# Attention with softmax sums by DMA: K and Q copies one every two tiles, other tiles added by DMA, late raw weights two heads later

## The chip, the cores and the metric

The kernel runs on one core of one Trainium2 chip. The metric is the device time of one execution in microseconds. An engine is named as in the profile: PE is TensorE, DVE VectorE, ACT ScalarE, POOL GpSimd, SP SyncE, which here only issues DMAs.

## The reference

The output mixes two branches on the same input x (2048 tokens, 1024 features) by a gate per token. Branch A is attention with 32 heads of 32 features; branch B picks one expert of 64 for each of 32 router heads. All inputs are float32.

```python
x = A_x
g = _sigmoid((x * gate_w).sum(-1, keepdims=True))
a = _A_ref(x, A_wqkv, A_wo)
b = _B_ref(x, B_w_q, B_k1, B_k2, B_u, B_v)
return g * a + (1 - g) * b

def _A_ref(x, wqkv, wo):
    qkv = (lambda x, *d: x.transpose(*d))((x @ wqkv).reshape(B, S, 3, H, Dh), 2, 0, 3, 1, 4)
    q, k, v = qkv[0], qkv[1], qkv[2]
    scores = jnp.einsum("bhqd,bhkd->bhqk", q, k) * (Dh ** -0.5)
    p = _softmax(scores, axis=-1)
    o = jnp.einsum("bhqk,bhkd->bhqd", p, v)
    return (lambda x, *d: x.transpose(*d))(o, 0, 2, 1, 3).reshape(B, S, D) @ wo
```

## The kernel before

The program has three stages. Up to about 630 us it computes Q and K (stored to DRAM as a high and a low part), the router, the branch of the experts and the values. From there to about 1630 us it runs attention, head by head. The last 180 us multiply the heads' results by wo, with the gate, and store the output. The change touches attention only.

**One head.** A head h has 16 key tiles (kt 0 to 15) of 128 keys; a tile P[h, kt] holds exp of the scores of these keys against all 2048 queries, 128 x 2048 float32, 1 MB. Scores are matmuls of K and Q tiles of 98 rows (three parts of 32 rows and a shift of 2 rows), 512 queries each, into a ring of seven PSUM banks (line 1284). ScalarE takes exp from the ring into P (line 1296). Then `pv` multiplies P by the values into O[h] (line 1308). These run in batches: 9 or 10 score matmuls, then four or five half tiles of products, seven pairs of them in a head. The third batch of a head is the only one of ten.

**The sums of a softmax row** need all 16 tiles added up and then summed over the partitions. `presum(h, kt)` adds one tile: VectorE adds most of them into ACC[h] (line 1342, two halves of 1024 columns each), and the tiles named in `SUMS` go into ACCD[h] instead, the first of them by being written there (ACCD[h] is that P tile itself), the others by an accumulating DMA that GpSimd issues (line 1330). Such a DMA waits for the tile, for the one before it into the same ACCD, and the first of a head also until the products have read the tile that ACCD is. `merge4` adds ACC and ACCD on VectorE. For the first 24 heads (`FOURS` = 6 groups of four), `fold4` and `fold4_end` then add quarters of 32 partitions onto each other by GpSimd's DMAs, so that T (the tile rb) holds four heads in its four quarters, and `head_sums` sums a whole group over the partitions with one set of matmuls into the ring (line 1321). From head 24 on pairs are folded instead of fours, by one DMA for each head.

**Buffers.** ACC and ACCD have two buffers each. P tiles have 11 places at first; from a given call of `p_tile` on 9, then 8, since the last three places are tiles (wo_raw3, wo_raw2, vhl) that later hold weights for the last stage. `PLACES` names the calls, `LATE` the heads at which those weights are loaded, `until` is a guess of when a place comes free, by which the next place is chosen.

**The order of the work.** Instructions are written out by hand for each engine; an engine takes its own in order, and starts one when what it depends on is done. `at(step, f)` puts a call into the list `todo` of a step; step h * 16 + kt is reached in the program after the batch in which the scores of that tile are complete, and the step's list comes ahead of that tile's `presum`. SP issues nearly all plain DMAs in program order, each on one of eight semaphores in turn, so it also waits until the DMA eight before has landed. In a head it issues the six copies of 32 rows of K and Q and the shift for the next head (`load_head`, 256 KB a copy, from DRAM into the buffer that the head before used), the store of O (`finish`, od<-osb), a part of the values (`load_v`), and in some heads a raw weight of wo (`load_wo`, 256 KB). After a group of four it also stores the sums (smd<-ssb, four DMAs), loads them again (`load_r`, rr<-smd) and stores their reciprocals (`norm_r`, rd<-rr).

The steps around the change, counted from a head's step 0: K and Q of the next head at -1; store of the head before at 0; merge of the head before at 3, its first folds at 5, its last at 10, and the rowsum of the group that ended two heads before at 2. Adds by DMA at 3, 8 and 12.

Of the kernel before, what the change touches and what calls it, by code (L numbers as in the profile page):

```python
# [19 lines left out]
H = 32  # L20
KC = D // 128
HC = KC // 2
NT = S // 128
# [9 lines left out]
def gated_mha_peer_kernel(ctx, tc, xT, wqkv, wv, wo, wq, k12, ug, v, out):  # L33
# [48 lines left out]
    def dma(dst, src, queue=nc.sync):  # L82
        a, b = (ap.bitcast(F32) if ap.dtype == F32R else ap for ap in (dst, src))
        return queue.dma_start(a, b)
# [179 lines left out]
        evac_hi(*args)  # L264
        evac_lo()

    def load_kq(h, tiles):
        K, Q = tiles
        rows = slice(32 * h, 32 * h + 32)
        (qh, ql), (kh, kl) = (tuple(t[rows, :] for t in parts) for parts in QKD)  # L270
        for tile_, srcs in ((K, (kh, kh, kl)), (Q, (qh, ql, qh))):
            for i, src in enumerate(srcs):
                dma(tile_[32 * i:32 * i + 32, :], src)

    def load_shift(h, tiles):
        dma(tiles[1][96:98, :], SHD[h])
# [429 lines left out]
    for blk, (k, n) in enumerate(order):  # L706
        w, c = chunks[k]
        t = pairs[k % 2]
# [441 lines left out]
    P, pools, keep = {}, {}, None  # L1150


    SUMS = (1, 3, 8, 12), (2, 4, 6)
    PLACES = (11, 0), (9, 28 * 11), (8, 28 * 11 + 12 * 9)
    LATE = 21, 28
    until = [0] * PLACES[0][0]

    def p_tile(h, kt):


        n = [places for places, k in PLACES if pools["next"] >= k][-1]
        pools["next"] += 1
        i = min(range(n), key=lambda i: until[i])
        until[i] = h * NT + kt + (14 if kt in SUMS[h == H - 1] else 4)
        pool, name = ((pools["right"], f"P{i}") if i < 4 else (pools["left"], f"P{i}") if i < 8 else
                      (keep, ("vhl", "wo_raw2", "wo_raw3")[i - 8]))
        P[h, kt] = pool.tile([128, S], F32, name=name)
        return P[h, kt]
# [102 lines left out]
    def scores(s0, s1):  # L1271


        n = s1 - s0
        banks = ring_banks(n)
        cuts = {c for c in range(1, n + 1) if c == n or (s0 + c) % NQ == 0 or banks[c] == 0}
        cuts |= set(range(1, max(1, n - NB) + 1))
        if n <= 2 * NQ:
            cuts |= {c + 2 for c in range(NQ, n, NQ) if not cuts & {c + 1, c + 3}}
        c0 = 0  # L1280
        for c, i in enumerate(banks):
            (h, kt), qc = divmod((s0 + c) // NQ, NT), (s0 + c) % NQ
            K, Q = KQ[h % 2]
            on_ring(nc.tensor.matmul(ring[:, i, :], K[:98, kt * 128:(kt + 1) * 128],  # L1284
                                     Q[:98, qc * 512:(qc + 1) * 512], start=True, stop=True), i)
            if c + 1 not in cuts:
                continue
            m = c + 1 - c0
            q0 = qc + 1 - m
            if q0 == 0:  # L1290
                if kt == SUMS[h == H - 1][0]:
                    P[h, kt] = ACCD[h] = wk.tile([128, S], F32, name="accd")
                else:
                    p_tile(h, kt)
            i -= m - 1
            on_ring(nc.scalar.activation(  # L1296
                P[h, kt][:, q0 * 512:(q0 + m) * 512].rearrange("p (a m) -> p a m", a=m),
                ring[:, i:i + m, :], AF.Exp, scale=SCALE), *range(i, i + m))
            c0 = c + 1
# [23 lines left out]
                                       start=(src is srcs[0]), stop=(src is srcs[-1]))  # L1323

    def presum(h, kt):
        sums = SUMS[h == H - 1]
        if kt == 0 or kt == sums[0] or (h == H - 1 and kt >= NT - 2):
            return
        if kt in sums:
            nc.gpsimd.dma_start(ACCD[h], P[h, kt], accum_op=OP.add)  # L1330
            return
        if kt == 1 + (sums[0] == 1):
            if h > 0:
                ACC[h] = wk.tile([128, S], F32, name="acc")
            add(ACC[h], P[h, 0], P[h, kt])
        else:
            add(ACC[h], ACC[h], P[h, kt])

# [131 lines left out]
    def at(step, f, *a):  # L1470
        todo.setdefault(step, []).append((f, a))

    for h in range(H):
        base = h * NT
        g, j = divmod(h, 4)
        if h >= 1 and h + 1 < H:
            at(base - 1, load_head, h + 1)
        if h < H - 1:
            at(base + NT, finish, h)
            if h == H - 2:  # L1480
                at(base + NT + 5, merge, h)
                at(base + NT + 8, head_sums, h)
            elif g < FOURS:
                at(base + NT + 3, merge4, h)
                at(base + NT + 5, fold4, h)
                at(base + NT + 10, fold4_end, h)
            else:
                at(base + NT + 3, (merge_even, merge_odd)[h % 2], h)
                at(base + NT + 5, (fold_even, fold_odd)[h % 2], h)
                if h % 2:  # L1490
                    at(base + NT + 12, head_sums, h - 1, 2)
        if j == 3 and g + 1 < G:
            if g < FOURS:
# [335 lines left out]
```

## Time and profile before

| | us |
|---|---|
| three runs | 1816.46, 1820.94 (median), 1826.25 |
| the profiled execution, its own time | 1816.36 |
| its span, first to last instruction | 1814.6 |
| an ordinary head of attention | 31.0 |
| attention, 32 heads | about 1000 |
| the last stage after it | about 180 |

The profile is of one execution. Its groups are named by line, engine and out<-in with the program's names: ring<-z,z and ring<-Q,K are scores, P<-ring their exp (into the places wo_raw and vhl too), o<-P,V the products, acc<-acc,P VectorE's adds, accd<-P the adds by DMA, rb<-acc,accd and acc<-acc,accd the merge, acc<-acc, rb<-acc and rb<-rb at lines 1384 to 1393 the folds, z<-kdh and K<-kdh (and qdh, kdl, qdl) the copies of K and Q. Queue q0 carries GpSimd's DMAs, q1 those of SP. PE is busy for 99% of the span, so where time can be won or lost is seen in the few stretches in which it isn't.

### The profile page before, as it was taken

What the parts mean: (1) busy time and instruction counts of PE and PEld (TensorE: products, weight loads), DVE (VectorE), ACT (ScalarE), POOL (GpSimd) and SP (SyncE); (2) the same over time, 40 slices, a digit from 0 to 9 for tenths busy, and PEclk for the clock granted to TensorE, in tenths of its full rate; (3) what the DMA queues carried; (4) which work ended last, traced back from release to release, by engine and by line L of the source; (5) the groups of instructions that cost most, each with busy time, mean ns of one, the idle gap of its engine ahead of it and who ended that gap; (6) DMA issues with size and microseconds to landing.
All of it is one profiled execution on the core that took longest, in us unless ns stands there. A gap on an engine that the chain in (4) does not pass through costs nothing.

```text
span 1814.6 us, 28137 instructions
## 1 busy us (share of the span) xinstructions
PE 1803.1 (99%) x10631; PEld 1137.4 (63%) x10631; DVE 1499.4 (83%) x1673; ACT 1221.6 (67%) x1615; POOL 261.4 (14%) x314
## 2 busy tenths in 40 slices
PE   9999999999999999999999999999999999999999
PEld 7777777788888754455554545554454555547887
DVE  7868785368987789998999998899889999995674
ACT  4434422211243499999999999999998999993221
POOL 0222000026401211111111111111111110101000
PEclk9999999999999999999999999999999999999999
DMA  7788888723248689999999999999998998967851
GB/s 240 235 283 259 265 264 306 252 70 106 82 144 275 228 195 201 192 191 204 196 212 194 213 191 204 184 205 193 184 219 172 204 204 191 207 141 236 272 167 58
DMA packets 132226, 364.74 MB, mean 201 GB/s; under 512 B 17541, under 2 KB 57877, under 8 KB 106169
## 3 DMA queue, kind: packets, MB, share of 16 engines
q0 software_dynamic: 22064, 136.07, 37.9%
q1 hardware_dynamic: 89864, 190.94, 34.7%
q10 hardware_dynamic: 20160, 35.92, 7.0%
q8 instruction: 84, 1.38, 0.3%
q14 instruction: 54, 0.43, 0.1%
HBM read 169.14 MB, written 72.10 MB: 133 GB/s over the span
## 4 chain that ended last, share of the span: by engine, by line
PE 91%; DMA 5%; DVE 2%; issue 1%; ACT 0%; SPq 0%; POOL 0%; ACTq 0%; DVEq 0%; POOLq 0%
PE ring L1284 25%; PE o L1308 22%; PE bk L157 13%; PE bk L713 10%; PE pa L157 6%; PE bk L760 5%; PE pa L1573 2%; PE bk L928 2%; DMA accd<-P 2%; PE bk L313 2%; PE bk L493 1%; DVE acc L1342 1%; DMA rb<-acc 1%; PE pa L1580 1%; PE bk L397 1%
## 5 line engine op out<-in xcount | busy, mean ns | idle before, releaser
L1296 ACT ACTIVATE P<-ring 128x512 f32<-128x512 f32 (+3 forms) x895 | 730.8, 939 | 12.9 <-PE ring L1284 4.9
L1342 DVE TENSOR_TENSOR acc<-acc,P 128x1024 f32<-128x1024 f32 x508 | 583.6, 1217 | 4.9 <-ACT P L1296 4.7
L1308 PE MATMUL o<-P,V 128*32 128x512 f32 (+1 forms) x3624 | 378.0, 531 | 0.0
L1284 PE MATMUL ring<-Q,K 98*128 98x512 f32 x1024 | 270.6, 407 | 3.3 <-ACT P L1296 3.3
L1284 PE MATMUL ring<-z,z 98*128 98x512 f32 x1020 | 267.7, 406 | 0.1
L1284 PEld LDWEIGHTS ring<-Q,K 98*128 98x128 f32 x1024 | 182.8, 188 | 124.6 <-issue 36.6
L1284 PEld LDWEIGHTS ring<-z,z 98*128 98x128 f32 x1020 | 182.1, 188 | 116.2 <-issue 39.9
L1308 PEld LDWEIGHTS o<-P,V 128*32 128x32 f32 x3624 | 100.4, 109 | 191.2 <-issue 171.1
L1330 POOL DMA_DIRECT2D accd<-P x81 | 72.1, 891 | 505.8 <-ACT P L1296 237.4
L1296 ACT ACTIVATE wo_raw<-ring 128x512 f32<-128x512 f32 (+3 forms) x144 | 114.2, 864 | 3.0 <-PE ring L1284 1.6
L1342 DVE TENSOR_TENSOR rb<-acc,accd 32x1024 f32<-32x1024 f32 (+2 forms) x60 | 70.7, 1217 | 54.4 <-DMA accd<-P 29.5
L242 ACT ACTIVATE hi<-bk 128x512 fp32r<-128x512 f32 x40 | 23.7, 595 | 114.2 <-PE bk L713 95.2
L713 PE MATMUL bk<-xh,e 128*128 128x512 f32 x384 | 94.2, 394 | 0.0
L713 PE MATMUL bk<-xl,e 128*128 128x512 f32 x384 | 92.2, 389 | 0.0
L1296 ACT ACTIVATE vhl<-ring 128x512 f32<-128x512 f32 (+3 forms) x106 | 85.5, 872 | 2.1 <-PE ring L1284 0.7
L713 PEld LDWEIGHTS bk<-xh,e 128*128 128x128 f32 x384 | 71.0, 188 | 22.0 <-issue 3.4
L255 DVE TENSOR_TENSOR lo<-bk,hi 128x512 fp32r<-128x512 f32 x40 | 27.5, 689 | 66.8 <-ACT hi L242 61.6
L713 PEld LDWEIGHTS bk<-xl,e 128*128 128x128 f32 x384 | 72.1, 188 | 15.0
L1342 DVE TENSOR_TENSOR acc<-acc,wo_raw 128x1024 f32<-128x1024 f32 x68 | 79.8, 1218 | 0.3 <-ACT wo_raw L1296 0.3
L103 DVE TENSOR_TENSOR e<-wraw,e 128x512 fp32r<-128x512 f32 (+3 forms) x64 | 54.8, 864 | 28.3 <-ACT e L102 27.7
L1342 DVE TENSOR_TENSOR acc<-acc,vhl 128x1024 f32<-128x1024 f32 x62 | 72.9, 1217 | 0.0
L102 ACT ACTIVATE e<-wraw 128x512 fp32r<-128x512 f32 (+3 forms) x64 | 44.7, 705 | 39.1 <-DMA wraw<-in_wqkv 23.4
(305 smaller groups left out, 2550.2 us busy)
## 6 DMA issues: line engine op xcount, KB each, us to landing
accd<-P POOLq DMA_DIRECT2D x81, 1024.0 KB, 11.2
wqt<-in_wq SPq DMA_DIRECT2D x26, 1024.0 KB
wraw<-in_wqkv SPq DMA_DIRECT2D x30, 512.0 KB
rb<-acc POOLq DMA_DIRECT2D x36, 256.0 KB, 7.9
accd<-wo_raw POOLq DMA_DIRECT2D x9, 1024.0 KB, 10.2
qdh<-hi ACTq DMA_DIRECT2D x32, 256.0 KB
qdl<-lo ACTq DMA_DIRECT2D x32, 256.0 KB
kdh<-hi ACTq DMA_DIRECT2D x32, 256.0 KB
```

The lines of the kernel that those rows point to most:

```text
L102: nc.scalar.activation(hi, src, AF.Copy)
L103: (on or nc.vector).tensor_tensor(out=lo, in0=src, in1=hi.bitcast(F32), op=OP.subtract)
L157: nc.tensor.matmul(ps, self.a[a][i][:, k, :], self.b[b][j][k], start=(not first and k == 0 and i == j == 0), stop=(k == HC - 1 and i == 1))
L313: nc.tensor.matmul(ps[32 * quad:32 * quad + 32, :], kpad[:, quad % 2, i, :], t[:, quad, :], start=(i == 0), stop=(i == 3))
L713: nc.tensor.matmul(ps, t[:, kc // HC, a, kc % HC], x_at(b, n, kc), start=first, stop=last)
L760: nc.tensor.matmul(ps, x_at(a, t // 4, kc)[:, tok], b, start=first, stop=last)
L928: nc.tensor.matmul(p, x_at(a, t // 4, kc)[:, tok], b, start=first, stop=last)
L1284: on_ring(nc.tensor.matmul(ring[:, i, :], K[:98, kt * 128:(kt + 1) * 128], Q[:98, qc * 512:(qc + 1) * 512], start=True, stop=True), i)
L1296: on_ring(nc.scalar.activation(P[h, kt][:, q0 * 512:(q0 + m) * 512].rearrange("p (a m) -> p a m", a=m), ring[:, i:i + m, :], AF.Exp, scale ...
L1308: nc.tensor.matmul(O[h][32 * qc:32 * qc + 32, c0:c1], Vt[g][:, kt, 32 * j:32 * j + 32], p[:, qc * 512 + c0:qc * 512 + c1], start=(kt == 0) ...
L1330: nc.gpsimd.dma_start(ACCD[h], P[h, kt], accum_op=OP.add)
L1342: nc.vector.tensor_add(out[:, c], a[:, c], b[:, c])
```

## The change

- `load_kq` can issue single pieces. The six copies for the next head are put at steps -1, 1, 3, 5, 7 and 9 of a head and the shift at 10, in place of all seven at -1.
- For heads 1 to 30, `SUMS` is (0, 2, 6, 10): ACCD is tile 0, and tiles 2, 6 and 10 are added to it by DMA. Before it was tile 1 with 3, 8 and 12. Head 0 keeps (1, 3, 8, 12), head 31 keeps (2, 4, 6). ACC starts with the first two of the other tiles, now 1 and 3, before 0 and 2.
- Merge, first folds and last fold of a head go to steps 4, 6 and 11 of the next head, before 3, 5 and 10; the rowsum of a group of four stays. So the last fold comes after the third add of its head in GpSimd's order, where it came between the second and the third.
- The raw weights that were loaded in heads 21 to 28 are loaded in heads 23 to 30 (`LATE`), and the P tiles go from 11 places to 9 at call 338 of `p_tile` (in head 22) in place of 308 (in head 20).

```diff
-    def load_kq(h, tiles):
+    def load_kq(h, tiles, pieces=range(6)):
         K, Q = tiles
         rows = slice(32 * h, 32 * h + 32)
         (qh, ql), (kh, kl) = (tuple(t[rows, :] for t in parts) for parts in QKD)
-        for tile_, srcs in ((K, (kh, kh, kl)), (Q, (qh, ql, qh))):
-            for i, src in enumerate(srcs):
-                dma(tile_[32 * i:32 * i + 32, :], src)
+        places = [(t, i, src) for t, srcs in ((K, (kh, kh, kl)), (Q, (qh, ql, qh)))
+                  for i, src in enumerate(srcs)]
+        for n in pieces:
+            t, i, src = places[n]
+            dma(t[32 * i:32 * i + 32, :], src)
...
-    SUMS = (1, 3, 8, 12), (2, 4, 6)
-    PLACES = (11, 0), (9, 28 * 11), (8, 28 * 11 + 12 * 9)
-    LATE = 21, 28
+    SUMS = (1, 3, 8, 12), (0, 2, 6, 10), (2, 4, 6)
+    PLACES = (11, 0), (9, 338), (8, 28 * 11 + 12 * 9)
+    LATE = 23, 28
+
+    def sums_of(h):
+        return SUMS[(h > 0) + (h == H - 1)]
...
-        sums = SUMS[h == H - 1]
-        if kt == 0 or kt == sums[0] or (h == H - 1 and kt >= NT - 2):
+        sums = sums_of(h)
+        first, second = [t for t in range(NT) if t not in sums][:2]
+        if kt == first or kt == sums[0] or (h == H - 1 and kt >= NT - 2):
             return
...
-        if kt == 1 + (sums[0] == 1):
+        if kt == second:
             if h > 0:
                 ACC[h] = wk.tile([128, S], F32, name="acc")
-            add(ACC[h], P[h, 0], P[h, kt])
+            add(ACC[h], P[h, first], P[h, kt])
...
         if h >= 1 and h + 1 < H:
-            at(base - 1, load_head, h + 1)
+            for i in range(6):
+                at(base - 1 + 2 * i, load_kq, h + 1, KQ[(h + 1) % 2], [i])
+            at(base + 10, load_shift, h + 1, KQ[(h + 1) % 2])
...
             elif g < FOURS:
-                at(base + NT + 3, merge4, h)
-                at(base + NT + 5, fold4, h)
-                at(base + NT + 10, fold4_end, h)
+                at(base + NT + 4, merge4, h)
+                at(base + NT + 6, fold4, h)
+                at(base + NT + 11, fold4_end, h)
             else:
-                at(base + NT + 3, (merge_even, merge_odd)[h % 2], h)
-                at(base + NT + 5, (fold_even, fold_odd)[h % 2], h)
+                at(base + NT + 4, (merge_even, merge_odd)[h % 2], h)
+                at(base + NT + 6, (fold_even, fold_odd)[h % 2], h)
                 if h % 2:
-                    at(base + NT + 12, head_sums, h - 1, 2)
+                    at(base + NT + 13, head_sums, h - 1, 2)
```

In `p_tile` and `scores` the lookups `SUMS[h == H - 1]` become `sums_of(h)`.

More of the change, by code (lines that the diff above doesn't have):

```diff
@@ L1163, in p_tile @@
         i = min(range(n), key=lambda i: until[i])
-        until[i] = h * NT + kt + (14 if kt in SUMS[h == H - 1] else 4)
+        until[i] = h * NT + kt + (14 if kt in sums_of(h) else 4)
         pool, name = ((pools["right"], f"P{i}") if i < 4 else (pools["left"], f"P{i}") if i < 8 else
@@ L1290, in scores @@
             if q0 == 0:
-                if kt == SUMS[h == H - 1][0]:
+                if kt == sums_of(h)[0]:
                     P[h, kt] = ACCD[h] = wk.tile([128, S], F32, name="accd")
```

## The prediction

> **What bounds the kernel now.** I read the busy shares first, then the chain of work that ended last by engine, then windows of a head's length (an ordinary one and the worst), then the waits inside the worst.
>
> ```profile
> PE 1803.1 (99%) x10631; PEld 1137.4 (63%) x10631; DVE 1499.4 (83%) x1673; ACT 1221.6 (67%) x1615; POOL 261.4 (14%) x314
> PE 91%; DMA 5%; DVE 2%; issue 1%; ACT 0%; SPq 0%; POOL 0%; ACTq 0%; DVEq 0%; POOLq 0%
> 758.60:789.70 31.10, 31.10 (x223) 15.30 (x221) 28.29 (x25) 30.36 (x40) 5.15 (x7) 1.00 0.94 202
> 1350.20:1381.40 31.20, 27.91 (x184) 13.46 (x183) 25.02 (x23) 25.69 (x31) 4.90 (x6) 0.95 0.89 172
> ```
>
> TensorE is busy without a gap in an ordinary head (31.10 of 31.10 us, window row: length, PE, PEld, DVE, ACT, POOL, granted clock, DMA share). The change touches attention alone and removes no matmul, so it can only win back stalls. A usable clock for them is the third batch of scores, ten matmuls, once in every head; I call its start M. From the chain in order of time:
>
> ```profile
> 789.73 2.71 PE ring L1284 x10
> 945.74 2.59 PE ring L1284 x10
> 976.70 2.59 PE ring L1284 x10
> 1101.59 2.59 PE ring L1284 x10
> 1164.36 2.71 PE ring L1284 x10
> 1290.52 2.70 PE ring L1284 x10
> 1420.69 2.71 PE ring L1284 x10
> ```
>
> A head is 30.96 us (945.74 to 976.70). From 789.73 to 1164.36 are twelve heads, 374.63 us, 124.88 for four. The next four take 126.16 (1.28 more), the four after them 130.17 (5.29 more). So 6.57 us of stall is all there is to win in this execution. TensorE's two recorded waits, and the work before the longer:
>
> ```profile
> PE ring L1284 <- ACT P L1296: 3.3, 1, 3.3
> PE ring L1321 <- DMA rb<-acc: 0.8, 1, 0.8
> 1343.61 2.28 PE ring L1284 x9
> 1345.89 2.29 PE o L1308 x24
> 1350.06 12.19 DMA accd<-P
> 1362.35 2.36 DVE rb L1342 x2
> 1370.53 1.77 PE ring L1284 x4
> ```
>
> VectorE stood until 1362.35 at the merge of head 22, because the last accumulating DMA into accd landed late; P tiles came free late, ScalarE had no place to write, TensorE waited 3.3 us. The clock of 0.95 over that window is another 1.6 us (0.05 x 31.2). The 0.8 us is the rowsum of a group of four heads, waiting for its last fold.
>
> Why the DMA is late shows on the GpSimd queue and in the time to landing: in order the add of tile 12 of head 9; of head 10 the adds of tiles 3 and 8, the last fold of head 9's sums, and tile 12; then tile 8 of head 15.
>
> ```profile
> 934.26 0.89 POOL L1330 DMA_DIRECT2D accd<-vhl  x1 [6.50 <-ACT P L1296]
> 945.87 0.86 POOL L1330 DMA_DIRECT2D accd<-P  x1 [10.73 <-ACT P L1296]
> 957.63 0.90 POOL L1330 DMA_DIRECT2D accd<-P  x1 [6.20 <-ACT wo_raw L1296]
> 960.28 0.78 POOL L1393 DMA_DIRECT2D rb<-acc  x1 [1.76 <-DMA rb<-acc]
> 965.85 0.90 POOL L1330 DMA_DIRECT2D accd<-P  x1 [4.78 <-PE ring L1284]
> 1112.76 0.92 POOL L1330 DMA_DIRECT2D accd<-P  x1
> ```
>
> ```profile
> accd<-vhl POOLq DMA_DIRECT2D x1, 1024.0 KB, 7.2
> accd<-P POOLq DMA_DIRECT2D x1, 1024.0 KB, 11.2
> accd<-P POOLq DMA_DIRECT2D x1, 1024.0 KB, 7.7
> accd<-P POOLq DMA_DIRECT2D x1, 1024.0 KB, 10.9
> accd<-P POOLq DMA_DIRECT2D x1, 1024.0 KB, 13.9
> ```
>
> The 7.2 is of 934.26, 11.2 of 945.87, 7.7 of 957.63, 10.9 of 965.85, 13.9 of 1112.76. The three adds of a head go into one tile, so each waits for the one before: M+0.1 to M+11.3, M+11.9 to M+19.6, M+20.1 to M+31.0 in head 10, which fills the head. In head 15 the second one is behind late folds and lands at M+25.1 (1126.7). A late merge makes late folds, and these make the next merge late: it goes on so until the add of 1350.06 above, head 22's third, which takes 12.19 us.
>
> **The change, part by part.**
>
> *K and Q copies.* No bytes change. The rows of the SP queue around head 9 and of the DMA queues while an add ran alone and with the copies (932 to 940.4, 966 to 978):
>
> ```profile
> 902.80 0.89 SPq L84 DMA_DIRECT2D z<-kdh  x2
> 909.91 0.52 SPq L84 DMA_DIRECT2D od<-osb  x1
> 925.49 0.36 SPq L84 DMA_DIRECT2D rr<-smd  x1
> 937.71 0.32 SPq L84 DMA_DIRECT2D rd<-rr  x1
> 938.07 2.33 SPq L84 DMA_DIRECT2D K<-kdh  x2
> ```
>
> ```profile
> q0 software_dynamic: 211, 1.47, 94.2%
> q0 software_dynamic: 161, 1.06, 50.0%
> q1 hardware_dynamic: 354, 1.62, 46.6%
> ```
>
> The step numbers pace nothing: SP issues a copy as soon as its waits are met. In the new order only the first copy goes out at the head's start; the other five stand behind the store of o, which waits for ScalarE, 7.1 us later (902.80 to 909.91), and then leave together. So the copies are moved by 5 to 7 us, not spread. That still helps one place: before head 10 the copies were held behind rd<-rr until 938.07, and the add of tile 12 landed in 7.2 us; before head 11 they went out with it and it took 10.9. Gain: 3.7 us at the end of each chain. Loss: the first add of the next head meets five copies; it met the tail of six already and took 11.2. Bounds of that loss: 0 (as now) to 3.7 (all given back); I take 0, as the nearest row is 11.2 with copies in flight.
>
> The Trainium skill, page "DMA: Bandwidth & Descriptors", section "Queues, rings and completion order", says that each DMA engine takes turns between the queues it has work for, packet by packet. The 50.0 and 46.6% agree. By that rule the copies cost the same wherever they meet an add, the loss is 3.7 and the chain is no shorter: a rival below.
>
> In the heads after a group of four, two copies also stand behind rr<-smd (925.49, M(9)+10.8, with M(9) 914.6 by the 31.1 us before 945.74). They must land before the next head's scores, which start 9.2 us before M (two batches and two products at 2.3), at 936.5: 11 us of cover, and 10.9 is what an add of twice their bytes took while it shared the engines. I cost it at nothing; without cover it costs TensorE directly.
>
> *Tiles 2, 6, 10 into tile 0.* Three adds by DMA and eleven by VectorE, as before: no bytes, no instruction more. Tile 0's products come one tile ahead of tile 1's, so the first add goes out at M or up to a tile earlier; I take M. Tiles 6 and 10 exist two tiles earlier (a tile is 30.96/16 = 1.9 us), so only the landings set the chain: M to 11.2; 11.7 to 19.4; 19.9 to 27.1 (7.2) or 30.8 (10.9). The merge, moved a tile later, stands at about M'+1.9 less what VectorE waited, M' being M+31.0: the landing has 3.9 us and more in hand where it had none.
>
> What is late next is the last fold. It was issued before the add of tile 12 (960.28, M+14.5); now it comes after that of tile 10 on GpSimd, at M+20.8 (19.9 and 0.9 for the issue), and not before.
>
> ```profile
> DMA to landing us min/median/max: 5.6/7.7/10.7
> DVE rb L1342 <- DMA accd<-P: 29.5, 10, 6.1
> ```
>
> It lands (first row, all 23 recorded last folds) at M+28.5, between 26.4 and 31.5; the rowsum of a group needs it at M+31.0, in TensorE's order just ahead of the ten. Cover 2.5 us, at worst 0.5 short, six groups: 0 to 3 us, I take 2. Behind the same fold stands VectorE's first add of the next head, since acc has two buffers; it has about as much cover, its wait is taken up by the P places, and it replaces the wait of the second row.
>
> *One-tile shifts of merge and fold* go with the above: TensorE has no work in them. *Late raw weights:* eight loads of 256 KB move from heads 21 to 28 into 23 to 30, after the four-head folds end at 24, and eleven P places last until mid head 22 instead of mid head 20. Cost nothing: first use is in head 31. They remove pressure from heads 21 and 22; head 23, where the 3.3 us fell, still has nine places and is saved only if its merge is in time.
>
> **Sum.** Own time of the profiled execution 1816.36, less 1.28, less 5.29, plus 2: 1811.8, I say 1812. The median shown is 1820.94, 4.6 above this execution; whether its extra time is more of the same stalls no row shows. Against the median, 1812 is 0.49% less. A run of this kernel can tell about 0.5% from no change, so faster means under 1811.8, slower over 1830.0.
>
> **Rivals.** *Conserved:* what the last add gains the first one loses, the late regime remains, later raw weights save little: 1814 to 1821, say 1817. For it: the shared queues, and that the copies are not spread. Against: the 7.2 of 934.26, followed by only 11.2.
>
> *The last fold stalls the rowsum (slower):* if the second add lands as in head 15, M+25.1, the fold goes out at M+26.5 and, at the 7.7 above, lands M+34.2: 3.2 us of idle TensorE per group, six groups 19, with the clock's share (half as much again by the 1.6 on 3.3) 29: 1809.8 plus these is 1829 to 1839, say 1834. It decides from a second add landing later than M+21.9 (31.0 less 7.7, 0.9 and 0.5). For it: the 0.8 us wait of exactly this kind, and the late adds from head 15 to head 22. Against: a stall gives the chain its time back, so the next group starts in time.
>
> *K and Q late* after a group: the two copies 3 us past 936.5 in seven heads, 21 us: 1831. Against it the 11 us of cover.
>
> **How the numbers follow.** Forecast 0.55, of which 0.40 under 1811.8 (runs with less than 2 us left) and 0.15 above; conserved 0.20; fold 0.18, of which 0.15 over 1830; late copies 0.07. Faster 0.40, same 0.38, slower 0.22. The forecast's own range is 1809 to 1815; the range asked for reaches over the conserved case and the milder half of the fold's: 1808 to 1829.
>
> **What would show it.** Right: merges no longer wait for accd, the last add of a head lands in about 7 us, four-head distances between M stay at 124.9 throughout, no clock below 1.00 in attention, od before five copies on SP. Wrong: waits of L1321's counterpart on the fold, second adds landing after M+22, K or Q named as what ended a TensorE wait, or a first add of 14 us or more.

## The result, and the profile after

The changed kernel takes 1934.05 us (median of 6 runs, 1929.45 to 1943.86) against 1820.94 us (6 runs, 1816.46 to 1826.25): a ratio of 1.0625, 95% interval 1.0595 to 1.0656. It is slower by 113 us, where 9 less were forecast, and the range ended at 1829. The profiled execution has a span of 1932.4 us.

From the profile page of the changed kernel, busy shares and the chain that ended last by engine; then, from that chain in order of time, the third score batch (the ten matmuls that the prediction uses as a clock; start, length):

```profile
PE 1837.4 (95%) x10631; PEld 1148.4 (59%) x10631; DVE 1501.6 (78%) x1673; ACT 1225.1 (63%) x1613; POOL 261.9 (14%) x314
PE 79%; DMA 11%; issue 3%; DVE 3%; ACT 2%; SPq 1%; POOL 0%; ACTq 0%; DVEq 0%; POOLq 0%
```

```profile
844.61 2.59 PE ring L1290 x10
875.57 2.59 PE ring L1290 x10
950.20 4.57 PE ring L1290 x10
984.25 2.60 PE ring L1290 x10
...
1126.62 2.60 PE ring L1290 x10
...
1269.93 2.59 PE ring L1290 x10
```

DMA is on the chain for 11% where it was 5%, and TensorE is idle for 95 us of the span (1932.4 less 1837.4), where it was 11.5. For the same 10631 matmuls it is also busy 34 us longer (1803.1 before). An undisturbed head still takes 30.96 us (844.61 to 875.57). But four heads, from one of these to the next after a group, take 139.64, 142.37 and 143.31 us (844.61, 984.25, 1126.62, 1269.93), where the prediction had 124.88. These groups of four lose 15 to 18 us each, and the six groups together are nearly all of the 113 us. Two heads lie between 875.57 and 950.20, 74.63 us, so the loss falls at the end of the group; and the batch of 950.20 took 4.57 us, where 2.59 is usual.

The waits of the changed kernel (engine, line, what it waited for: total us, times, longest), TensorE's and then VectorE's:

```profile
PE ring L1327 <- issue: 40.5, 4, 10.3
PE ring L1327 <- DMA rb<-acc: 19.8, 2, 11.6
PE ring L1290 <- ACT P L1302: 19.4, 13, 5.4
```

```profile
DVE acc L1349 <- ACT P L1302: 87.2, 32, 12.3
DVE acc L1349 <- DMA rb<-acc: 28.0, 6, 7.2
```

Line 1327 is the rowsum, line 1290 the scores. The rowsum of a group waits six times, once for each group, about 10 us each, 60.3 in all: before, 0.8 once. VectorE waits six times for the DMA rb<-acc, the last fold, a wait that it did not have; and scores wait for P places 13 times. Where did one of the 10 us come from? GpSimd's queue and TensorE around the group that ends with head 7 (its folds run in head 8, from 897.3; the rowsum is due in head 9), start, length, and in brackets the idle time before and what ended it; then the time from issue to landing of the DMAs issued at 906.12, 924.19 and 938.54, in that order:

```profile
906.12 0.90 POOL L1337 DMA_DIRECT2D accd<-wo_raw  x1 [1.95 <-ACT P L1302]
...
924.19 1.48 POOL L1337 DMA_DIRECT2D accd<-P  x1
938.00 0.86 POOL L1337 DMA_DIRECT2D accd<-wo_raw  x1 [12.33 <-DMA accd<-P]
938.54 1.13 POOL L1400 DMA_DIRECT2D rb<-acc  x1
```

```profile
accd<-wo_raw POOLq DMA_DIRECT2D x1, 1024.0 KB, 16.6
...
accd<-P POOLq DMA_DIRECT2D x1, 1024.0 KB, 13.2
...
rb<-acc POOLq DMA_DIRECT2D x1, 256.0 KB, 9.5
```

```profile
948.26 1.94 PE L1327 MATMUL ring<-rb,ones 128*32 128x512 f32 x8 [10.31 <-issue]
950.13 4.64 PE L1290 MATMUL ring<-Q,K 98*128 98x512 f32 x10
```

```profile
948.30:957.00 8.70, 8.70 (x34) 4.11 (x38) 8.70 (x8) 5.50 (x6) 0.85 (x2) 0.50 0.72 160
```

Head 8's M is 906.5 (its ten matmuls in the trace). Its first add takes 16.6 us, its second 13.2 and lands at 937.4, M+30.9 (the prediction: M+19.4). The third add and, 0.54 us behind it, the last fold go out at once; the fold lands at 948.0 and the rowsum, due at 937.9, starts at 948.26. The ten matmuls behind it take 4.64 us instead of 2.6. From 948.3 to 957.0 the granted clock is 0.50 (the window row above: length, PE, PEld, DVE, ACT, POOL, clock, DMA share, GB/s), so these 8.7 us do the work of 4.35: the stall costs 4.4 us more than its length, and such stretches are where the 34 us of longer busy time come from. What ended the wait is the DMA, though the profile's word for this one is "issue".

### The profile page after: what moved, and what is told of

Its sections match the earlier page's. It is cut to its first block, busy times and chain, and to the rows that moved or that the text cites. A ratio compares the mean times of both kernels' runs of the same rounds, so it can differ in the third digit from the quotient of the medians.

```text
span 1932.4 us, 28115 instructions
## 1 busy us (share of the span) xinstructions
PE 1837.4 (95%) x10631; PEld 1148.4 (59%) x10631; DVE 1501.6 (78%) x1673; ACT 1225.1 (63%) x1613; POOL 261.9 (14%) x314
## 4 chain that ended last, share of the span: by engine, by line
PE 79%; DMA 11%; issue 3%; DVE 3%; ACT 2%; SPq 1%; POOL 0%; ACTq 0%; DVEq 0%; POOLq 0%
PE ring L1290 21%; PE o L1314 18%; PE bk L157 12%; PE bk L715 9%; PE pa L157 6%; PE bk L762 5%; DMA rb<-acc 4%; PE bk L930 2%; DVE acc L1349 2%; PE bk L315 2%; DMA accd<-wo_raw 1%; DMA accd<-P 1%; ACT P L1302 1%; PE pa L1582 1%; PE bk L495 1%
## 5 line engine op out<-in xcount | busy, mean ns | idle before, releaser
L1302 ACT ACTIVATE P<-ring 128x512 f32<-128x512 f32 (+3 forms) x911 | 759.7, 951 | 51.4 <-DVE acc L1349 25.9
L1349 DVE TENSOR_TENSOR acc<-acc,P 128x1024 f32<-128x1024 f32 x548 | 629.9, 1219 | 11.4 <-ACT P L1302 11.2
L1314 PE MATMUL o<-P,V 128*32 128x512 f32 (+1 forms) x3784 | 398.2, 538 | 0.0
L1290 PE MATMUL ring<-Q,K 98*128 98x512 f32 x1024 | 279.6, 418 | 1.5 <-ACT P L1302 1.0
L1349 DVE TENSOR_TENSOR acc<-P,P 128x1024 f32<-128x1024 f32 x58 | 68.5, 1222 | 143.3 <-ACT P L1302 59.9
L1337 POOL DMA_DIRECT2D accd<-P x59 | 55.5, 941 | 404.7 <-ACT P L1302 140.0
L1302 ACT ACTIVATE wo_raw<-ring 128x512 f32<-128x512 f32 (+3 forms) x108 | 100.2, 997 | 0.8 <-PE ring L1290 0.5
L1327 PE MATMUL ring<-rb,ones 128*32 128x512 f32 x72 | 14.7, 902 | 60.2 <-issue 40.5
L1302 ACT ACTIVATE accd<-ring 128x512 f32<-128x512 f32 (+1 forms) x100 | 65.3, 741 | 8.7 <-PE ring L1290 8.6
L1302 ACT ACTIVATE vhl<-ring 128x512 f32<-128x512 f32 (+3 forms) x70 | 67.9, 1030 | 4.0 <-PE ring L1290 3.8
## 6 DMA issues: line engine op xcount, KB each, us to landing
accd<-wo_raw POOLq DMA_DIRECT2D x23, 1024.0 KB, 11.9
```

The lines of the kernel that those rows point to most:

```text
L1302: on_ring(nc.scalar.activation(P[h, kt][:, q0 * 512:(q0 + m) * 512].rearrange("p (a m) -> p a m", a=m), ring[:, i:i + m, :], AF.Exp, scale ...
L1314: nc.tensor.matmul(O[h][32 * qc:32 * qc + 32, c0:c1], Vt[g][:, kt, 32 * j:32 * j + 32], p[:, qc * 512 + c0:qc * 512 + c1], start=(kt == 0) ...
L1349: nc.vector.tensor_add(out[:, c], a[:, c], b[:, c])
```

## The experiments

Eighteen kernels, each beside runs of the kernel before on the same chip (medians 1816 to 1818 us), in the order of the questions.

| run | us (runs) | ratio, 95% interval |
|---|---|---|
| e6 changed kernel, copies and last fold as before | 1819.59 (8) | 1.0018, 0.9979 to 1.0057 |
| e4 before, late raw weights alone | 1818.06 (10) | 1.0002, 0.9970 to 1.0034 |
| e1 changed, last fold ahead of the third add | 1848.89 (2) | 1.0167, 1.0121 to 1.0214 |
| e2 changed, copies as before | 1893.87 (2) | 1.0415, 1.0367 to 1.0462 |
| e3 before, copies of the change alone | 1861.65 (2) | 1.0238, 1.0172 to 1.0303 |
| e14 before, last fold behind the third add alone | 1907.36 (4) | 1.0480, 1.0441 to 1.0519 |
| e10 changed, rowsums read another tile | 1909.06 (2) | 1.0511, 1.0428 to 1.0593 |
| e11 e2, the last fold reads T | 1860.64 (4) | 1.0238, 1.0202 to 1.0275 |
| e7 e1, copies ahead of the sums' DMAs | 1862.13 (4) | 1.0240, 1.0170 to 1.0310 |
| e8 before, late copies ahead of the sums' DMAs | 1861.15 (4) | 1.0248, 1.0180 to 1.0316 |
| e15 before, no copies | 1809.31 (4) | 0.9949, 0.9925 to 0.9974 |
| e16 e8, half of the copies | 1810.16 (5) | 0.9957, 0.9940 to 0.9973 |
| e17 before, one copy twice | 1835.37 (7) | 1.0083, 1.0056 to 1.0111 |
| e12 before, early raw weights later | 1815.87 (12) | 0.9993, 0.9974 to 1.0012 |
| e13 e6, early raw weights later | 1817.49 (12) | 1.0001, 0.9978 to 1.0024 |
| e18 before, two adds by DMA in five heads | 1816.15 (12) | 0.9994, 0.9973 to 1.0014 |
| e19 before, two copies by GpSimd | 1867.41 (6) | 1.0274, 1.0239 to 1.0309 |
| e20 before, two copies by VectorE | 1830.30 (9) | 1.0075, 1.0050 to 1.0099 |

From the traces of these runs, medians over heads 1 to 24 of the time from issue to landing, in us, and where the merge stands after the start of its head's first score matmul:

| | first add | second | third | last fold | merge |
|---|---|---|---|---|---|
| before | 11.4 | 8.8 | 11.6 | 7.7 | 11.6 |
| changed | 16.5 | 10.3 | 8.4 | 9.9 | 18.2 |
| e1 | 14.0 | 8.7 | 8.0 | 7.9 | 11.0 |
| e2 | 12.4 | 8.7 | 10.5 | 12.1 | 14.1 |
| e3 | 14.0 | 9.1 | 8.0 | 8.3 | 10.2 |
| e8 | 16.4 | 9.9 | 10.3 | 7.4 | 17.5 |
| e11 | 11.9 | 7.8 | 10.9 | 12.7 | 11.0 |
| e15 | 8.9 | 7.4 | 7.4 | 7.3 | 8.3 |

### Which part costs: e6, e4, e1, e2, e3

e6 puts the copies and the last fold of the changed kernel back; tiles 2, 6, 10, the later merge and the late weights stay. e1 puts only the fold back, e2 only the copies.

```diff
-            for i in range(6):
-                at(base - 1 + 2 * i, load_kq, h + 1, KQ[(h + 1) % 2], [i])
-            at(base + 10, load_shift, h + 1, KQ[(h + 1) % 2])
+            at(base - 1, load_head, h + 1)
...
-                at(base + NT + 11, fold4_end, h)
+                at(base + NT + 10, fold4_end, h)
```

> The changed kernel with both undone: copies at step -1 and the last fold at step 10; tiles 2, 6, 10, the later merge and the late raw weights stay. Theory A and theory B both expect it near the kernel before, 1808 to 1830. If it is above 1860, the early tiles or the later merge are the cause and both theories fall.

> The changed kernel with the last fold of a head put at step 10 of the next head in place of 11, so that GpSimd issues it ahead of the third add again; all else as changed. Theory A (the fold behind the third add is what stalls the rowsum of a group and VectorE's next sum): the rowsum waits go, 10 us and the half clock after each of six groups at least, and the time falls from 1934 to 1815 to 1840. Theory B (the copies of K and Q, moved behind the store of o, meet the first add and the folds and make the chain of three adds longer than a head): the first adds still land 14 to 19 us after issue, the merges still slip from T+11 to T+24 over a group, and the time stays above 1870.

> The changed kernel with all seven copies of K, Q and shift back at step -1; other tiles, the shifted steps and the late raw weights stay. Theory A: the last fold still goes out behind the third add, about 30 us after the head's start, and lands 8 to 10 us into the head after, so rowsums still wait and the time stays above 1870. Theory B: first adds land in 11 us again, the chain fits into a head, the last fold lands before the rowsum, and the time is 1812 to 1835.

e4 is the kernel before with `PLACES` 338 and `LATE` 23 of the change, e3 the kernel before with `load_kq` by pieces and the copies' steps of the change (the first four lines of the diff above, the other way round).

> The kernel before with only the raw weights two heads later and eleven P places until call 338. If the stalls of heads 21 and 23 come from the nine places, 3 to 6 us less than before; if from the late merges alone, the same time within 3 us.

> The kernel before with nothing changed but the copies, one every two steps. Theory A: the old fold order keeps 7 us in hand, so the time is 1815 to 1835. Theory B: the first add meets the copies, the chain outgrows the head, merges slip and P places run out: above 1860.

e6 and e4 can't be told from the kernel before. So the tiles, the shifted merge and the weights together make no difference that these runs can tell (e6: between 0.2% less and 0.6% more), and the loss lies in the other two: putting the fold back wins 85 us of the 113, putting the copies back 40, both 114. They overlap by about 11 us.

In e1 and in e3 the adds' chain is in step (merge at 11.0 and 10.2), and most of the loss lies around the heads after a group: 17 of TensorE's 24 us of waits in e1's attention, and 31 of 35 in e3's, are one wait after each of the six groups. The waits of TensorE in e1, and, in e3, SyncE's issues and TensorE around the head after the second group:

```profile
PE ring L1290 <- DMA z<-qdh: 10.4, 4, 3.8
PE ring L1290 <- DMA z<-shd: 6.7, 2, 4.8
PE ring L1290 <- DMA K<-kdh: 4.6, 1, 4.6
```

```profile
924.55 4.60 SPq L84 DMA_DIRECT2D smd<-ssb  x4
...
937.50 0.35 SPq L84 DMA_DIRECT2D rr<-smd  x1
937.90 0.43 SPq L84 DMA_DIRECT2D z<-qdl  x1
938.37 0.43 SPq L84 DMA_DIRECT2D V<-vd  x1
938.84 0.51 SPq L84 DMA_DIRECT2D z<-qdh  x1
939.39 1.45 SPq L84 DMA_DIRECT2D z<-shd  x1
```

```profile
945.18 0.61 PE L1310 MATMUL o<-wo_raw,V 128*32 128x256 f32 x8
951.29 4.18 PE L1286 MATMUL ring<-z,z 98*128 98x512 f32 x9 [5.50 <-DMA K<-kdh]
```

The head starts at 913.8, its M is 923.8. rr<-smd goes out at M+13.7, not at M+10.9 as in the kernel before: it must wait for the four smd<-ssb, and these are through SyncE only at 929.15 (M+5.4; before, M+2.9 in the trace), with copies ahead of them and in flight. The next head's scores were due at 945.8; what stands behind rr<-smd is ready only at 951.29, and TensorE stood 5.5 us. From this M to the next it takes 39.8 us instead of 31.1. (The scores read z; the profile names a K copy of the same moment.) The V load between the copies shows why the copies issued at 938 to 941 came so late. The DMA queues from 942 to 944 in e3, packets, MB and share:

```profile
q0 software_dynamic: 48, 0.39, 94.2%
q1 hardware_dynamic: 48, 0.02, 6.2%
```

48 packets of the adds' queue and 48 of SyncE's in the same time: they alternate. The former hold 8 KB each, the latter 512 bytes (0.39 MB and 0.02 MB over 48), so the V load and the z copy behind it crawl as long as DMAs of the adds' queue run. The Trainium skill, page "DMA: Bandwidth & Descriptors", section "Queues, rings and completion order", has this rule, a packet in turn from each queue. This trace agrees, and shows that a turn is no equal share of bytes. The kernel before agrees as well, from 968 to 975, while the add of 965.85 meets the copies of head 11:

```profile
q0 software_dynamic: 112, 0.92, 72.3%
q1 hardware_dynamic: 112, 0.66, 26.3%
```

The packets are equal in number, the shares of time are not. The prediction's 50.0 and 46.6% (966 to 978) look equal only because the copies ran on alone once the add's packets had ended: its rows have 161 packets against 354. That the V load is what holds the z copy is read from this trace; it was not tried by itself.

### The last fold: e14, e10, e11

e14 is the kernel before with one number changed, so that the fold stands behind the add of tile 12:

```diff
-                at(base + NT + 10, fold4_end, h)
+                at(base + NT + 13, fold4_end, h)
```

> The kernel before with the last fold issued behind the third add of its head (tile 12) instead of ahead of it; nothing else. Theory (this order alone costs, whichever tiles are added by DMA): 1870 to 1900 us, first adds of a head still 11 us, rowsum stalls of about 10 us in the groups. Rival (it costs only together with tiles 2, 6, 10 and the later merge): under 1835 us.

1907 us, above the range, with the changed kernel's picture: waits of TensorE and VectorE.

```profile
PE ring L1321 <- issue: 41.5, 4, 11.9
PE ring L1321 <- DMA rb<-acc: 18.8, 2, 11.6
```

```profile
DVE acc L1342 <- DMA rb<-acc: 68.6, 10, 9.4
```

So the order alone does it, whichever tiles are added. Two things wait for that fold: TensorE's rowsum and, through acc's two buffers, VectorE's first sum of the next head. e10 takes the first away (a group's rowsum reads a tile of values instead of T, so the sums of these heads are left out), e11 the second (in e2, the last fold adds a quarter of T instead of one of acc, so that acc is free after the first folds).

```diff
-        for ins in rowsum(ring[:, i, :], T if heads > 1 else ACC.pop(h),
+        for ins in rowsum(ring[:, i, :], Vt[h // 4 + 1].rearrange("p t m -> p (t m)") if heads == 4
+                          else T if heads > 1 else ACC.pop(h),
...
-        src = T[quarter(1)] if q == 0 else ACC.pop(h)[others(q)[0]]
+        src = T[quarter(1)] if q == 0 else T[others(q)[0]]
```

> The changed kernel, but the rowsum of a group of four reads a V tile in place of the folded sums, so it waits for no fold (the softmax sums of these heads are left out). Theory A1 (the wait of the rowsum is the loss by the fold): six times 10 us and their half clock go, 1934 falls to about 1850. Theory A2 (the late fold also holds VectorE's next sum, so merges, folds and P places slip further, and the stall of the rowsum was what let the chain catch up): the merges keep slipping past T+25, TensorE stalls on P places instead, and the time stays above 1890.

> The changed kernel with its copies back at the head's start (the run that gave 1894 us), and besides the last fold of each group-of-four head adds a quarter of T to T in place of a quarter of acc: the same bytes, the same place behind the third add, but the buffer of acc is free after the first folds. The softmax sums of heads 0 to 23 are wrong so. Theory (the late fold does its harm on VectorE: the next head's sum waits for acc's buffer, P places run out and merges slip, and the 10 us stalls at the rowsum follow from that): 1825 to 1845 us, no wait of VectorE for rb<-acc, merges steady near 11 us into the head, rowsum waits of 1 to 4 us in six groups. Rival (the fold's place in GpSimd's queue behind the third add is what costs, whoever waits for acc): 1880 to 1900 us with rowsum stalls of 10 us still there.

Without the rowsum's wait the changed kernel still takes 1909 us: only 25 of the 113 come back, and the K and Q copies become what TensorE waits for (`Q<-shd`, 31.3 us in three waits). Without VectorE's wait 33 of e2's 77 us come back (1893.9 to 1860.6), not the 50 to 70 that I expected: both accounts hold in part. The merges stay at 11.0 us (median), and the rowsum's stalls shrink from 10 to about 5 us, 27.5 in all, but do not vanish. TensorE's waits for the rowsum in e2 and in e11, and one group's end in e11: the third add and last fold issued in head 8 (start 879.0, M 888.1), their landing, and the rowsum:

```profile
PE ring L1327 <- issue: 40.1, 4, 12.3
PE ring L1327 <- DMA rb<-acc: 21.0, 2, 13.3
```

```profile
PE ring L1327 <- issue: 19.4, 4, 5.3
PE ring L1327 <- DMA rb<-rb: 8.1, 2, 4.4
```

```profile
909.01 0.86 POOL L1337 DMA_DIRECT2D accd<-wo_raw  x1 [7.11 <-ACT P L1302]
909.55 1.13 POOL L1400 DMA_DIRECT2D rb<-rb  x1
```

```profile
accd<-wo_raw POOLq DMA_DIRECT2D x1, 1024.0 KB, 13.5
rb<-rb POOLq DMA_DIRECT2D x1, 256.0 KB, 14.7
```

```profile
924.43 1.93 PE L1327 MATMUL ring<-rb,ones 128*32 128x512 f32 x8 [5.26 <-issue]
926.29 4.63 PE L1290 MATMUL ring<-Q,K 98*128 98x512 f32 x10
```

This is the fold's own cost, with the chain otherwise in step. It goes out at M+21.4, close to where the prediction put it (M+20.8), and lands 14.7 us later (median of all heads 12.7) instead of 7.7. What sets the landing is the add ahead of it on the queue, which here lands at 922.5 (909.01 and 13.5): the fold follows 1.7 us later. That is so in every kernel here. In the kernel before the fold goes out 1.3 to 8.6 us (median 3.0) behind the second add and lands 0.9 to 3.6 us (median 1.9) after it; in e11 and e14 it goes out 0.5 us (median) behind the third add and lands 2.3 and 1.9 us (medians) after that one.

### The late copies: e7, e8, e15, e16, e17

If the two copies behind rr<-smd were all, issuing them ahead of the sums' DMAs should bring the time back. e7 does so in e1, e8 in the kernel before:

```diff
-            at(base - 1, load_head, h + 1)
+            at(base - 1, load_kq, h + 1, KQ[(h + 1) % 2], [0])
+            at(base + 1, load_kq, h + 1, KQ[(h + 1) % 2], range(1, 6))
+            at(base + 1, load_shift, h + 1, KQ[(h + 1) % 2])
```

> The changed kernel with the last fold at step 10, and with the five later copies and the shift all at step 1: still behind the store of o, but ahead of the stores and the load of a group's sums (smd, rr) on SP. If what is left of e1_fold_first's loss is the two copies that stand behind rr<-smd in the heads after a group, its heads of 34 to 40 us go back to 31.9 and the time falls from 1849 to 1808 to 1822. If the shared first adds cost time by themselves, it stays above 1835.

> The kernel before with only the copies moved, in the same way: one at step -1, five and the shift at step 1. By the same reasoning e3_copies_only's loss of 44 us is the wait behind rr<-smd and goes: 1808 to 1825. If late copies lengthen the chain of adds (first adds 14 us in place of 11), merges slip and it stays above 1835.

It did not: 1862 and 1861 us. The head after a group is back at 32 us, and no wait for K or Q is left; but now the adds slip (e8: first add 16.4 us, merge at 17.5) and scores wait for P places. The waits of TensorE in e7:

```profile
PE ring L1290 <- ACT P L1302: 29.4, 13, 6.4
```

In e1 and e3 the stall after each group had given the chain its time back. That left two accounts: the bytes of the copies, or their order on SyncE. e15 leaves all copies and the shift out from head 2 on, e16 is e8 with K's three copies alone (one early, two late), e17 is the kernel before with each head's first copy done twice:

```diff
-            at(base - 1, load_head, h + 1)
+            pass
...
+            at(base - 1, load_kq, h + 1, KQ[(h + 1) % 2], [0])
+            at(base + 1, load_kq, h + 1, KQ[(h + 1) % 2], [1, 2])
...
+            at(base - 1, load_kq, h + 1, KQ[(h + 1) % 2], [0, 1, 2, 3, 4, 5, 0])
+            at(base - 1, load_shift, h + 1, KQ[(h + 1) % 2])
```

> The kernel before without any copy of K, Q and the shift from head 2 on (scores of stale K and Q; the attention part is wrong so). 1.5 MB a head less on the DMA engines. Theory (engines full, adds pay for the copies): 1806 to 1813 us, first and third adds of a head land 8 to 10 us after issue in place of 11, no wait of the merge. It also gives the floor that any placing of the copies could reach.

> The kernel with only the copies late (1861 us) and of each head's copies only K's three: one early, two late behind the store of o; Q's three and the shift are left out, so the scores are wrong. Theory 1 (bytes): first adds 11 to 12 us, 1808 to 1825 us. Theory 2 (order on SP): 1840 us or more.

> The kernel before with the first copy of each head done twice, all at the old place: 256 KB a head more. Theory 1 (engines full, 5 per cent or 1.6 us a head left, and 256 KB take about 1.3 us of all engines at the 200 GB/s of the windows): the late stretch of heads 14 to 23 comes earlier and is deeper, 1825 to 1850 us. Theory 2: 1816 to 1820 us.

All three came out as the account by bytes has it. e16 takes away bytes and late issues together, so it doesn't tell the two apart by itself; and e8 loses with the same bytes as the kernel before, so their place counts as well. The window from 660 to 790 us holds about four heads, in which none of these kernels stalls yet. Its rows in e15, in the kernel before and in e17 (window, PE, PEld, DVE, ACT, POOL, granted clock, DMA share, GB/s):

```profile
660.00:790.00 130.00, 130.00 (x912) 65.61 (x909) 119.75 (x105) 127.56 (x163) 20.17 (x24) 1.00 0.73 144
```

```profile
660.00:790.00 130.00, 130.00 (x910) 65.38 (x907) 118.96 (x104) 127.54 (x164) 20.16 (x24) 1.00 0.96 198
```

```profile
660.00:790.00 130.00, 130.00 (x912) 65.69 (x909) 118.86 (x104) 127.55 (x164) 20.18 (x24) 1.00 0.98 207
```

The six copies fill 23 points of the DMA engines' time, 7 us of a head, and 4 points are left, 1.2 us. One copy more leaves 2 and costs 0.83%; three copies and the shift fewer win 0.43%, though two of the three that are left go out late. In the same window e8 has a share of 0.91 with all of the copies issued: placed late, they leave 5 points more of the engines' time unused, 1.5 us of a head, which is more than there was to spare. Worked out from the packets of heads 2 to 5 in stretches of 3 us from a head's start: in the kernel before the engines are full for the first 15 us (0.96 or more); in e8 they are at about 0.75 from 9 to 15 us, while the copies and the first add run together, and at about 0.45 from 24 to 27 us, about where the first add lands and the second goes out. So the head's traffic no longer fits into the head, and its adds run over into the next. Why the mixed stretch is less full is not settled.

### Looking for a faster kernel: e12, e13, e18, e19, e20

Three edits aimed at the kernel's own stalls of 6.6 us: e12 and e13 move the eight raw-weight loads of heads 8 to 15 to heads 24 to 27, e18 adds two tiles by DMA instead of three in heads 7, 11, 15, 19 and 23.

```diff
-            at(((8 if k < 4 else LATE[0] - 8) + 2 * k + j) * NT + 11, load_wo, kc, j)
+            at((24 + k) * NT + 12 + j if k < 4 else (LATE[0] - 8 + 2 * k + j) * NT + 11, load_wo, kc, j)
...
+        return SUMS[1 if h == H - 1 else 2 if h in (7, 11, 15, 19, 23) else 0]
```

> The kernel before with the eight raw-weight loads of heads 8 to 15 (256 KB each) moved into heads 24 to 27, behind the folds of four; nothing else. If these loads start the late stretch of heads 14 to 23 (6.6 us of stall in the profiled execution): 1808 to 1814 us, four-head distances of 124.9 throughout. If the late stretch comes from the folds alone: 1816 to 1820 us with the stretch still there. If the loads only carry the stretch on into heads 24 to 27: 1820 to 1830 us.

> The changed kernel with copies and last fold as before (tiles 2, 6, 10, later merge and late weights remain; it gave 1820 us) and the eight loads of heads 8 to 15 moved into heads 24 to 27. If the loads set off the late stretch of heads 7 to 13 in it: 1808 to 1814 us. If not: 1816 to 1822 us.

> The kernel before with two adds by DMA in place of three in heads 7, 11, 15, 19 and 23 (tile 12 is added by VectorE there). If the chain of adds is what runs late in heads 14 to 23: the stretch is gone, four-head distances of 124.9 throughout, 1808 to 1813 us, ratio 0.995 to 0.998. If VectorE, busy 94 per cent there, becomes the bound: 1820 us or more.

None differs from the kernel before. In the profiled executions e12 and e18 still stall between heads 17 and 24; e13 doesn't stall before head 28, but then waits 4.6 us for P places, behind the heads to which the loads were moved. What starts the late stretch stays open; taking away 2 MB of weights, or five of its adds, is not enough to win time.

Two edits aimed at the floor that e15 and e16 showed, 1809 to 1810 us, with all the work done. K holds kh twice and Q holds qh twice; the second is copied inside SBUF from the first, by GpSimd (e19) or VectorE (e20):

```diff
+    def same_rows(h):
+        K, Q = KQ[h % 2]
+        nc.gpsimd.tensor_copy(K[32:64, :], K[0:32, :])
+        nc.gpsimd.tensor_copy(Q[64:96, :], Q[0:32, :])
...
+            at(base + 4, same_rows, h + 1)
```

> The kernel before with two of each head's six copies (the second kh in K, the second qh in Q) made by GpSimd from the rows already loaded, behind the first add's issue: 512 KB a head less by DMA. Theory (DMA engines full): the merges stay near 8.5 us, four-head distances 124.9 throughout, 1808 to 1812 us, ratio 0.994 to 0.997. Rival (GpSimd's copies hold up its issues of folds and adds, or VectorE, long enough to give it back): 1815 us or more.

> The same two copies by VectorE, behind the merge. VectorE is busy 94 per cent of attention before (117.4 of 125 us), so about 1.9 us a head is free. If the two copies take 1 us each or less: 1808 to 1812 us. If they take 2 us each, VectorE becomes the bound: first adds and merges slip, 1820 to 1860 us.

The rivals won both times. A group of these copies in e19 (count, busy us, mean ns), then, also of e19, the merge's adds (ns, shortest, median, longest) and one of the first folds on GpSimd; a group of the copies in e20 and a window of it:

```profile
L1254 POOL CAST z<-z 32x2048 fp32r<-32x2048 f32 x12 | 65.7, 5476 | 0.5
```

```profile
L1348 DVE TENSOR_TENSOR rb<-acc,accd x58: 1207/1496/2912, 664.5 to 1599.6; 32x1024 f32<-32x1024 f32 x36, 128x1024 f32<-128x1024 f32 x18, 64x1024 f32<-64x1024 f32 x4
769.59 0.78 POOL L1393 DMA_DIRECT2D acc<-acc  x1 [3.76 <-DVE acc L1348]
```

```profile
L1254 DVE CAST z<-z 32x2048 fp32r<-32x2048 f32 x12 | 14.6, 1217 | 0.4
```

```profile
790.00:915.00 125.00, 125.00 (x873) 62.91 (x874) 124.41 (x111) 122.59 (x153) 21.88 (x24) 1.00 0.89 179
```

VectorE takes 1.22 us for a copy, and with two of them a head it is busy for 124.41 of 125 us: its merge slips to 13.9 us (median), and the adds behind it. GpSimd's copies are slower, 2.4 to 5.5 us by the mean of each group (spans on this engine are rough). They hold up VectorE rather than GpSimd's own issues: 42 of VectorE's adds in attention, 30 of them of the merge into rb, take 1.3 to 2.9 us, where none takes over 1.23 in the kernel before or in e20. All 42 run beside one of GpSimd's copies, and they lose 60 us in all. The first folds go out 0.3 us behind the merge's end in both kernels, and GpSimd stood 3.76 us for it in the row above; they go out 5 us later (median) because the merge starts later and takes longer. That the slow adds start this delay is read from the trace; no run takes it apart. No version was found that beats the kernel before with all of the work done.

## Why the prediction was wrong

**What bounds the kernel: right.** An undisturbed head stays at 30.96 us, and the time moves only through stalls. That 6.57 us at most could be won is borne out from the other side: without any copies (e15) the kernel takes 1809.3, 7.4 less than the 1816.7 of the kernel before beside it, and no score waits.

**Tiles 2, 6, 10, the shifted merge, late raw weights, at nothing: right.** e6 is 0.18% above the kernel before and e4 0.02%, neither to be told from none. The merge's "3.9 us and more in hand" doesn't follow from its own numbers, though: landings from M+27.1 to M+30.8 leave 2.1 to 5.8 us before M+32.9.

**The last fold, "lands at M+28.5": wrong, by the term of its landing.** The issue was right when the chain is in step (M+20.8 forecast, M+21.4 in e11's group above), the 7.7 us was not. It is no property of the fold: those of the kernel before went out a median of 3.0 us behind the second add and landed about 2 us after it. Moved behind the third add, the fold lands about 2 us after that one. The prediction had the third add landing between M+27.1 and M+30.8, so by its own numbers the fold lands between M+29 and M+33, from 2 us before the rowsum needs it to 2 us after. In e11's group above the add itself is later too, 13.5 us from issue to M+34.4, where 7.2 to 10.9 us were forecast, and the fold lands at M+36.1. No cover of 2.5 us, but a lack of 3.7 to 5.3 us in each of e11's six groups, with the merges in step. The sentence "0 to 3 us, I take 2" was to hold for all six groups.

**VectorE's first add behind the same fold, "taken up by the P places": wrong.** Scores hardly waited for P places in e2 (0.8 us), but the wait lets its merge slip from 11 us to 24 within a group, and the folds behind the merge with it. So the rowsum, which needs the last of them, waits 61.1 us in e2 and 27.5 in e11, where acc is free sooner: about the 33 us between the two kernels. In the changed kernel P places run out as well, 19.4 us in 13 waits.

**The copies, "I take 0": half right on the adds, wrong on what stands behind.** The gain of the last add came (11.6 to 8.0 us in e3, 3.7 forecast), the loss of the first is 2.6 us (11.4 to 14.0), within its bounds of 0 to 3.7 but not at the end that I chose. On the chain of e3 the two nearly cancel, which is the rival "Conserved". What cost the time in e1 and e3 is the term costed at nothing for its "11 us of cover": I took the issue of rr<-smd from the kernel before (M+10.8), while in e3 the stores of the sums, with copies ahead of them on SyncE, move it to M+13.7, and I took the landing from an add's 10.9, while the copies stand behind a V load whose 512-byte packets alternate with 8 KB ones.

**What the prediction had no term for** is how little slack the DMA engines have. I read 0.94 for the busy window and did not turn it into time: 4 to 5% of a head is 1.2 to 1.5 us, and each of the two orders needed more. With the copies issued ahead of the sums (e7, e8) no wait for K or Q remained, and the loss was no smaller (2.4 and 2.5%).

**The rivals.** "The last fold stalls the rowsum" names the right mechanism and its condition (a second add later than M+21.9) is met in head 8, M+30.9; but it stalls in e11 too, with the second add in time (M+20.3 in head 8), and its price of 3.2 us a group is 10. "A stall gives the chain its time back" is right too: after each group's stall the next head is in step. It only doesn't help, since the following group builds up the same delay. "K and Q late" was right in kind, 21 us forecast, while e1 and e3, where most of the loss lies around the heads after a group, are 1.7 and 2.4% above the kernel before, some 30 and 43 us. Each of the signs named as "wrong" appeared: the rowsum's wait on the fold, second adds after M+22, K or Q behind a TensorE wait, and a first add of 14 us or more.

## What to carry to other kernels

A time from issue to landing belongs to what stood ahead on the queue: when a DMA is moved behind another, price it by the landing of that one, not by its own old median. Where DMA engines are as busy in a loop as here (0.94 to 0.96), turn the rest into us per iteration first; a reordering that moves no byte can need more than that. A wait that comes back every iteration has no cover in buffers, which only take it once; look for what resets it, and expect that a fix for the wait which did the resetting brings the slip to light.

## What the runs showed of the hardware

- A 256 KB accumulating DMA on GpSimd's queue landed about 2 us after the 1 MB one ahead of it (medians 1.9, 2.3 and 1.9 us in the kernel before, e11 and e14), whether it was issued 3.0 or 0.5 us behind (medians); so its own time from issue to landing was 7.7 or 12.7 us.
- Packets of the two DMA queues alternated one to one whatever their size: 48 of 8 KB and 48 of 512 bytes in the same 2 us (e3), 112 and 112 in 7 us of the kernel before, where the adds' queue took 72% of the time and SyncE's 26%.
- After an idle stretch of 5.3 us (e11) and of 10.3 us (changed kernel) the granted clock was 0.50 for another 8.2 and 8.7 us of matmuls: each of these stalls of TensorE cost about 4 us more than its length.
- The kernel before scatters between 1809.5 and 1829.3 us from run to run. Without the copies it stays within 0.7 us (1809.0 to 1809.7, 4 runs), with half of them within 1.5 (5 runs): the scatter goes away with the load on the DMA engines.
- Copying 32 x 2048 float32 inside SBUF took 1.22 us on VectorE and 2.4 to 5.5 us on GpSimd, by the mean of each group. Beside GpSimd's copies VectorE's adds of two SBUF tiles, 1.22 us otherwise, took up to 2.9 us (42 of them, e19).
